# Reordering VectorE's queue in a fused attention and two-layer kernel: evacuations ahead of left-over jobs, weight sums behind the next maximum

## The chip, the cores and the metric

The kernel runs on one core of a Trainium2 chip. The time is that of one execution on the device, in microseconds (us); every kernel was run several times and medians are quoted. TensorE is called PE, VectorE DVE, ScalarE ACT, GpSimd POOL, as in the profile.

## The reference, cut to what matters

```python
# q, k, v: (8, 12, 448, 64), fp32
q_n, k_n = rmsnorm(q, g_q), rmsnorm(k, g_k)
scores = q_n @ k_n.T / sqrt(64)
attn   = softmax(scores)                 # per row, with the row's maximum taken off
x      = (attn @ v), heads side by side  # 3584 x 768
h      = x @ w_in                        # 768 x 2048
out    = max(0.01*h, h) @ w_out          # 2048 x 768
```

The kernel works through 24 units (`u` = 0 to 23), each of four heads of one batch. A unit has four stages (`d` = 0 to 3): in each, some score products and exponentials, and pieces of the two dense layers of an earlier batch, taken from a queue, so that PE has work while ACT takes exponentials. The second dense layer computes most of its output blocks with seven products in place of eight; for that it needs sums of weight blocks (`tw`, made once) and sums of activation blocks (`sa`, made for every pair of output tiles).

## The kernel before: the parts that matter

Evacuations of the dense layers' PSUM banks (DVE or ACT reads a product's result out of the bank in which it was accumulated) are not emitted at once. They are put on a list (`later`) and emitted by `flush()`, which every piece calls first. A stage also has *jobs*, small pieces of work for other engines; one is emitted behind each piece of the queue, and what is left over comes at the end:

```python
def fill(u, d, jobs):
    ...                                   # how much of the queue this stage takes
    while queue and debt[0] >= queue[0][0] * 0.5:
        c, fn = queue.pop(0)
        fn()
        debt[0] -= c
        if jobs:
            jobs.pop(0)()
    for job in jobs:                      # left-over jobs
        job()
    flush()                               # then what is pending
```

The start of a unit (abridged). `shift_max` is the DVE maximum and the diagonal `dg` made of it, `shift_mm` the small product that spreads it:

```python
qk(u, STEPS[d])
if d == 0:
    shift_max(u)                          # DVE: L219, L221
    if narrow(u - 1):
        pv_slot(u - 1)                    # PE: L326
        zcol(u - 1)                       # PE: L269
        shift_mm(u)                       # PE: L231, needs dg; then DVE L232, L240
        pv_out(u - 1); zcol_sum(u - 1)    # ACT L281; DVE L286, L287
ex(u)                                     # ACT: L201
```

The jobs that the argument touches (abridged):

```python
if d == 1:  job(prep_ssq, u + 2, ...) x2                  # DVE L142
if d == 2:  job(prep_rinv, u + 2)                         # ACT L147, L148
            job(prep_norm, u + 2, ...) x2                 # DVE L154, q then k
            job(prep_trd, u + 2)                          # transpose by DMA
if d in (1, 3) and 4 <= u < 8:
    job(weight_sum, u - 4, d // 2)                        # DVE L402, two halves
```

And four of the seven products of an output block (abridged). Products 5 and 6 accumulate onto banks that DVE has to have read in between:

```python
def i4():
    flush(); mm(bank("md"), sa[:, 2], tw[:, 2], True)
    later(lambda: add(g["o"][1][:, R], g["o"][1][:, R], "md"))   # DVE reads md, L434
def i5():
    flush(); mm(g["mc"], sa[:, 3], wblock(1, 1), False)
    ...
def i6():
    flush(); mm(g["md"], gblock(tt[1], 1), tw[:, 3], False)      # onto md again
def i0(), i2():                                                   # the same with bank ma, read at L443
    ...
```

The softmax here doesn't subtract the row's maximum and nothing guards it: scores larger than these inputs give would overflow.

## Time and profile before

| | before |
|---|---|
| median of 3 runs | 433.38 us (433.32 to 433.84) |
| span in the profile | 431.2 us |
| PE busy | 409.3 us, 95% |
| ACT, DVE busy | 306.5 us (71%), 273.2 us (63%) |
| PE waiting for DVE's diagonal (L231) | 2.4 us, 4 times |
| PE waiting for DVE's read of `md` | 1.3 us, 4 times |

How to read it: PE is the bound nearly everywhere, so only gaps in PE's own row cost time. A line of the list of waits has the engine that waits with its line, whom it waits for, then total us, number, longest. A line of a timeline has start, duration, engine, line, operation, and in brackets the idle time ahead of it and what ended it. A matmul's end is modelled, so the bracket shows less than the real gap; the distance of two starts, compared with the same pair elsewhere, shows it fully. The lines themselves stand in the prediction.

### The profile page before, as it was taken

The page shows a single profiled execution, that of the slowest core. Times are in us where ns is not written, and L with a number is a line of the kernel's source. Part 1 is how long each engine was busy: PE and PEld are TensorE (multiplying, and loading weights), DVE is VectorE, ACT ScalarE, POOL GpSimd, SP SyncE. Part 2 cuts the span into 40 slices and gives each one's busy share as a digit, 9 for nine tenths or more (in the row PEclk, how much of TensorE's full clock was granted, in tenths as well). Part 3 has the DMA queues.
Part 4 walks back from the last instruction along what each step waited for, and adds up shares of the span by engine and source line. Part 5 has one row for each costly group of instructions (what it writes and reads, how often), then busy time and mean ns, then how long its engine had stood idle before and what let it go on. Part 6 is the DMA issues. An engine that isn't in the chain of part 4 may idle for free.

```text
span 431.2 us, 8844 instructions
## 1 busy us (share of the span) xinstructions
PE 409.3 (95%) x3645; PEld 211.2 (49%) x3645; DVE 273.2 (63%) x434; ACT 306.5 (71%) x466; POOL 86.6 (20%) x77
## 2 busy tenths in 40 slices
PE   7677999999989999999999999999999999999996
PEld 6545444445444544454445544454445444455553
DVE  5898656888659865487369864587359840542162
ACT  5389888757986779966986789966986757643400
POOL 2885423300002102112102102111101101010000
PEclk9699999999999999999999999999999999999999
DMA  8999993789566896578555797488572460212013
GB/s 264 198 239 252 237 254 85 143 170 221 154 104 114 194 206 161 143 128 212 156 103 136 170 209 171 130 141 194 160 109 44 118 143 16 44 38 73 2 44 103
DMA packets 66476, 62.37 MB, mean 145 GB/s; under 512 B 35716, under 2 KB 61572, under 8 KB 66436
## 3 DMA queue, kind: packets, MB, share of 16 engines
q1 hardware_dynamic: 55840, 49.62, 46.7%
q0 software_dynamic: 10272, 11.80, 17.8%
q8 instruction: 28, 0.46, 0.4%
q10 hardware_dynamic: 324, 0.39, 0.3%
q14 instruction: 12, 0.10, 0.1%
HBM read 45.61 MB, written 11.01 MB: 131 GB/s over the span
## 4 chain that ended last, share of the span: by engine, by line
PE 63%; ACT 16%; DVE 12%; issue 3%; ACTq 0%; DVEq 0%
PE hps L347 25%; ACT et L201 8%; PE ma L427 7%; PE md L427 6%; PE sT L182 5%; PE sT L326 4%; PE op L387 4%; PE mc L427 4%; DVE n L154 3%; PE mb L427 3%; ACT gt L341 3%; PE zc L269 3%; DVE ssq L142 1%; DVE sT L219 1%; ACT x L281 1%
## 5 line engine op out<-in xcount | busy, mean ns | idle before, releaser
L201 ACT ACTIVATE et<-sT,eb 128x896 f16<-128x896 f32 x166 | 158.6, 1005 | 15.6 <-PE sT L182 13.3
L347 PE MATMUL hps<-xt,win 128*128 128x448 f16 x756 | 151.0, 353 | 0.2 <-DVE xt L335 0.2
L347 PEld LDWEIGHTS <-win 128*128 128x128 f16 x756 | 70.6, 98 | 71.4 <-issue 9.9
L341 ACT ACTIVATE gt<-hps 128x448 f16<-128x448 f32 x126 | 65.7, 541 | 20.1 <-PE hps L347 19.4
L306 POOL TENSOR_TENSOR xt<-x,rz 128x896 f16<-128x896 f32 x16 | 33.5, 2092 | 150.8 <-DMA rz<-zs 49.8
L154 DVE TENSOR_TENSOR n<-rq,rinv 128x896 f16<-128x896 f32 (+2 forms) x25 | 27.5, 1102 | 48.4 <-ACT rinv L148 44.9
L182 PE MATMUL sT<-qkT 64*64 64x448 f16 x664 | 52.6, 366 | 4.8 <-ACT et L201 4.3
L142 DVE TENSOR_REDUCE ssq<-sq 128x14 f32<-128x896 f32 (+2 forms) x49 | 50.1, 1055 | 1.2 <-ACT sq L131 1.2
L427 PEld LDWEIGHTS <-sa 128*128 128x128 f16 x352 | 32.8, 98 | 26.3 <-issue 6.1
L281 ACT COPY x<-sT 128x896 f32<-128x896 f32 x19 | 17.2, 907 | 39.5 <-DVE sT L232 39.5
L111 POOL DMA_DIRECT2D vt<-in_v_dram x24 | 18.2, 760 | 114.4 <-PE sT L326 106.9
L427 PEld LDWEIGHTS <-gt 128*128 128x128 f16 x264 | 25.2, 98 | 20.3 <-issue 4.4
L219 DVE TENSOR_REDUCE sT<-sT 128x1 f32<-128x896 f32 x22 | 24.0, 1093 | 17.5 <-PE sT L182 17.5
L182 PEld LDWEIGHTS <-qkT 64*64 64x64 f16 x672 | 15.8, 104 | 39.0 <-issue 35.9
L387 PE MATMUL op<-wout,gt 128*128 128x384 f16 x192 | 34.1, 327 | 0.0
L427 PE MATMUL ma<-wout,gt 128*128 128x384 f16 x176 | 32.3, 326 | 0.1
L154 DVE TENSOR_TENSOR n<-rk,rinv 128x896 f16<-128x896 f32 (+2 forms) x25 | 30.1, 1206 | 0.0
L326 PE MATMUL sT<-et,vt 64*64 64x448 f16 x532 | 28.5, 349 | 0.3
L408 DVE TENSOR_TENSOR sa<-gt 128x512 f16<-128x512 f16 (+1 forms) x15 | 8.1, 543 | 29.6 <-ACT gt L341 29.6
L326 PEld LDWEIGHTS <-vt 64*64 64x64 f16 x672 | 20.4, 107 | 10.8 <-issue 1.1
L387 PEld LDWEIGHTS <-gt 128*128 128x128 f16 x192 | 17.7, 98 | 14.0 <-issue 3.2
L453 ACT COPY ost<-ma 128x384 f32<-128x384 f32 x11 | 5.3, 480 | 23.6 <-PE ma L427 23.6
(87 smaller groups left out, 444.9 us busy)
## 6 DMA issues: line engine op xcount, KB each, us to landing
rq<-in_q_dram SPq DMA_DIRECT2D x24, 448.0 KB, 5.0
rk<-in_k_dram SPq DMA_DIRECT2D x24, 448.0 KB, 5.9
out_dram<-ost SPq DMA_DIRECT2D x52, 192.0 KB, 3.8
rz<-zs SPq DMA_DIRECT2D x38, 224.0 KB, 3.3
vt<-in_v_dram POOLq DMA_DIRECT2D x24, 224.0 KB, 5.0
win<-in_moe_w_in_dram POOLq DMA_DIRECT2D x8, 384.0 KB, 9.4
wout<-in_moe_w_out_dram POOLq DMA_DIRECT2D x2, 1536.0 KB, 23.7
out_dram<-ost SPq DMA_DIRECT2D x4, 96.0 KB, 2.1
```

Source lines behind the costliest of these rows:

```text
L142: nc.vector.tensor_reduce(buf(u, "ssq")[:, ti, :, c[0]:c[1]], buf(u, f"sq{ti}")[:, :, c[0]:c[1]], axis=AXL.X, op=ALU.add)
L154: nc.vector.tensor_tensor(buf(u, "n16")[:, ti, c[0]:c[1]].rearrange("p s a d -> p a s d"), src[:, :, c[0]:c[1]], buf(u, "rinv")[:, ti, :, ...
L182: nc.tensor.matmul(banks[a][64 * r:64 * r + 64, 0:S].rearrange("p (t x) -> p t x", t=NS), kT(u, r, a, t), qT(u, r, a), start=True, stop=True)
L201: nc.scalar.activation(s["et"][:, t], sT[:, :, 0:S], AF.Exp, bias=s["eb"], scale=1.0)
L219: nc.vector.tensor_reduce(s["spare"][:, 511:512], sT[:, :, 0:S], axis=AXL.XY, op=ALU.max)
L281: nc.scalar.copy(s["x32"], s["pslot"][:, :, 0:S])
L306: eng.tensor_tensor(xts[b][:, g], s["x32"], s["rz"], op=ALU.mult)
L326: nc.tensor.matmul(s["pv"][r][64 * a:64 * a + 64, 0:S], vts[u % NV][64 * r:64 * r + 64, a, t], s["et"][64 * r:64 * r + 64, t, a], start=(t ...
L341: nc.scalar.activation(dst, src, AF.Prelu, bias=0.0, scale=1.0, alpha=0.01)
L347: nc.tensor.matmul(hps[:, 0:S], win16[:, kt // 2, kt % 2, ts(ft, P)], xt[:, kt // 2, kt % 2], start=(kt == 0), stop=(kt == KT - 1))
L387: nc.tensor.matmul(op2[:, 0:HC], gt[:, ft, ds(col(t), P)], wout16[:, ft, ds(HC * half, HC)], start=(ft == 0), stop=(ft == FT - 1))
L427: nc.tensor.matmul(bank[:, 0:HC], a[:, f], b[:, f], start=(first and f == 0), stop=(f == HF - 1), skip_group_check=not first)
```

## The change

Its intent: DVE takes its queue in order, so what is emitted ahead of an urgent operation delays it. The change puts pending evacuations, on which PE may wait, ahead of left-over jobs, and takes half of each weight sum out of the place right ahead of the next unit's maximum.

```diff
@@ def fill
             if jobs:
                 jobs.pop(0)()
+        flush()
         for job in jobs:
             job()
-        flush()
@@ main loop
-                if d in (1, 3) and 4 <= u < 8:
-                    job(weight_sum, u - 4, d // 2)
+                if d == 1 and 4 <= u < 8:
+                    job(weight_sum, u - 4, 0)
+                if d == 0 and 5 <= u < 9:
+                    job(weight_sum, u - 5, 1)
```

## The prediction

> **What bounds the kernel now.** I read the page's busy shares first, then the list of who TensorE (PE) waits for, then the timelines of PE, VectorE (DVE) and ScalarE (ACT) around every PE wait. The page gives the bound:
>
> ```profile
> PE 409.3 (95%) x3645; PEld 211.2 (49%) x3645; DVE 273.2 (63%) x434; ACT 306.5 (71%) x466; POOL 86.6 (20%) x77
> PEclk9699999999999999999999999999999999999999
> PE 63%; ACT 16%; DVE 12%; issue 3%; ACTq 0%; DVEq 0%
> ```
>
> From slice 5 on PE is busy over 90%, its clock is full, and it leads the chain that ended last. The change adds and removes no instruction: the two programs have the same 7289 PE rows in the same order and the same DVE work in another order. It can only pay where PE now stands idle for DVE or ACT. That is this list:
>
> ```profile
> PE sT L182 <- ACT et L201: 4.3, 11, 0.9
> PE tp L610 <- DVE n L154: 3.7, 2, 3.0
> PE sT L231 <- DVE dg L221: 2.4, 4, 1.1
> PE md L427 <- DVE ost L434: 1.3, 4, 0.3
> ```
>
> The change touches only the last two lines. The first two are the prologue and the exponentials, whose order stays. L231 is the small product that spreads a unit's maximum, behind the DVE chain max (L219) then diagonal (L221). It stands behind that unit's first scores, the previous unit's PV and its column sums (L269). The two places where it waits long are the starts of units 6 and 8 (a unit is four heads of one batch, u = 0 to 23, in four stages):
>
> ```profile
> 89.64 0.85 PE L269 MATMUL zc<-et,onesr 128*32 128x448 f16 x16
> 91.29 0.22 PE L231 MATMUL sT<-dg,onesp 128*128 128x64 f16 x2 [0.81 <-DVE dg L221]
> 120.06 0.85 PE L269 MATMUL zc<-et,onesr 128*32 128x448 f16 x16
> 122.02 0.22 PE L231 MATMUL sT<-dg,onesp 128*128 128x64 f16 x2 [1.11 <-DVE dg L221]
> ```
>
> Matmul ends are modelled, so I take starts. Where nothing waits, L231 starts 0.78 us after L269 (138.08 to 138.86). So the real stalls are 91.29 - 89.64 - 0.78 = 0.87 us and 122.02 - 120.06 - 0.78 = 1.18 us. The same reading gives 0.12 us at unit 5 (76.86 to 77.76) and none at unit 7 (104.30 to 105.08).
>
> The fourth line is the last product of a seven-product output block. It accumulates into bank `md` that DVE must have read before:
>
> ```profile
> 149.85 1.47 PE L427 MATMUL mc<-wout,sa 128*128 128x384 f16 x8
> 151.64 1.46 PE L427 MATMUL md<-tw,gt 128*128 128x384 f16 x8 [0.32 <-DVE ost L434]
> 150.03 1.08 DVE L154 TENSOR_TENSOR n<-rk,rinv 128x896 f16<-128x896 f32 x1
> 151.03 0.55 DVE L434 TENSOR_TENSOR ost<-md,ost 128x384 f32<-128x384 f32 x1
> ```
>
> The DVE read ends at 151.58 and `md` starts at 151.64. Elsewhere the same pair of products starts 1.30 us apart (235.73 and 237.03), here 1.79, so the stall is 0.49 us. It occurs four times, at 151.6, 198.4, 295.1 and 345.2 (units 10, 13, 19, 22). The normalisation of k (L154) sits in front of the read only because it was emitted first.
>
> **What the Trainium skill says.** "Perfetto Trace Analysis", section "Identifying the Most-Contended Engine", says that matmul busy share does not measure the distance to the roofline, because matmuls are pipelined. The trace agrees: weight loads are 49% beside matmuls' 95%. So I count starts, not busy time. "PSUM — Partial Sum Buffer", section "Engine vs sequencer instructions", says that the queues of ScalarE, VectorE and GpSimd are strictly first in, first out and that matmuls start in program order; the `md` read behind L154 is just that. The same page, "PSUM bank collisions raise a hardware error", says that two engines must not touch one bank and quadrant at once; here `md` starts 0.06 us after the read ends. "SBUF — State Buffer", section "SBUF: two separate sides", says that GpSimd and a VectorE operation with two SBUF inputs share a port pair held for a whole instruction, and that the later one is fully blocked. The trace agrees: a weight sum (L402) takes 0.95 us alone but 1.66 us from 83.44 to 85.10, while GpSimd runs 82.61 to 84.29.
>
> **The change part by part.**
>
> (a) *Weight sums.* Eight instructions of 0.95 us (0.86 from start to next start). The four second halves leave the end of stage 3, ahead of the maxima of units 5, 6, 7 and 8, and go into stage 0 of those same units, after the maximum and the column-sum additions.
>
> Unit 5: the maximum goes from 76.29 to about 75.7, when its scores are ready, but L231 then waits for L269: gain 0.12 us.
>
> Unit 6: here DVE is the bound. From 80.62 to the diagonal at 90.95 its instructions stand practically back to back. The sum taken from 88.50 is balanced by the one now inserted at 81, in front of the same stretch. What is saved is only part of the port blocking: the sum at 83.44 starts 0.75 us later, GpSimd also moves, by 0.74 (its square waits for the reduction L142), and the sum ends at about 85.8 instead of 85.1. The maximum comes at 89.7 instead of 89.83. PE keeps nearly its whole 0.87 us stall. Units 5 and 6 together: 0.1 us.
>
> Unit 7: DVE had 0.51 us idle at 97.9 that takes up part of the insertion, and PE did not stall: 0.
>
> Unit 8: DVE is idle 4.27 us ahead of 115.21, so the sum inserted at 107 is free, and the one removed at 119.02 is a real saving:
>
> ```profile
> 115.21 1.09 DVE L154 TENSOR_TENSOR n<-rq,rinv 128x896 f16<-128x896 f32 x1 [4.27 <-ACT rinv L148]
> 119.02 0.95 DVE L402 TENSOR_TENSOR tw<-wout,tw 128x1536 f16<-128x1536 f16 x1
> 120.55 1.09 DVE L219 TENSOR_REDUCE sT<-sT 128x1 f32<-128x896 f32 x1
> ```
>
> The maximum moves to 119.69, the diagonal ends at about 121.1, L231 starts at about 121.16. Gain 0.86 us, with 0.32 of the 1.18 left. The fourth sum, now at about 124 in unit 8, falls into 4.02 us of DVE idle ahead of 129.45.
>
> (b) *Evacuations first.* In units 10, 13, 16, 19 and 22 the read of `md` now stands ahead of the normalisation of k. It starts about 1.0 us earlier (150.03) and ends at 150.6, before PE asks at 151.15. Four stalls of 0.49 us go: 1.96 us. Unit 16 has no such stall, since its `md` falls after the next maximum. The normalisation comes 0.46 us later, but feeds only a transpose for two units ahead.
>
> (c) *What the same edit costs.* In units 14 and 20 the pended sums of activations (L408, L411), which wait for ACT, now stand ahead of the second square reduction (L142, 1.00 us start to start), and so that reduction lies between them and the read of bank `ma`:
>
> ```profile
> 226.56 0.42 DVE L408 TENSOR_TENSOR sa<-gt 128x512 f16<-128x512 f16 x1 [3.08 <-ACT gt L341]
> 227.55 0.56 DVE L443 COPY ost<-ma 128x384 f32<-128x384 f32 x1
> 228.02 1.87 DVE L414 TENSOR_TENSOR sa<-gt 128x512 f16<-128x512 f16 x1
> ```
>
> The reduction would start at 227.35, the read at 228.35 and end at 228.90. PE wants `ma` again at 228.65: a stall of 0.3 us. Unit 8 shows that picture already: read 131.25, product 131.85 where 130.26 + 1.30 = 131.56 was due. Twice that is 0.6 us lost. The rest of the DVE delay vanishes: L414, 1.87 us long, is blocked by GpSimd until 229.6 anyway, so it ends at the same time, and the following maximum is not delayed.
>
> Sum: 0.1 + 0.86 + 1.96 - 0.6 = 2.3 us. 433.38 - 2.3 = 431.1.
>
> **The rivals.**
>
> *All four boundaries pay.* The naive count is that each removed sum moves its maximum by 0.86 us. For it: the chain of waits passes through L402 ahead of unit 6. Against it: the insertion into the same DVE-bound stretch, and no stall at unit 7. The most it could pay at unit 6 is its 0.87; then the time is about 430.3.
>
> *The delay is passed on.* In units 14 and 20 the reduction, moved out of 3.08 us of idle time into a busy DVE stretch, would delay the maxima of units 15 and 21 by up to 1.0 us each, if the GpSimd block did not absorb it. The profile shows the diagonal ready (235.56) only 0.1 us before PE wants it (235.66), so there is no room otherwise. Together with a gain at unit 8 that another wait takes over, the time would be about 433.
>
> *PE stalls vanish but ACT becomes the bound.* At units 10 and 22 ACT has over 2 us of idle time ahead of its next unit's first copy (2.74 us at 156.11), which speaks against it. It would leave about half of (b): 432.
>
> **Range and chances.** Each stall is counted directly and is small; no item alone can move the time by 2% (8.7 us), and all addressable stalls together are under 5 us. The three runs of before lie within 0.5 us. I take 430.2 to 432.4: the lower end is unit 6 paying too, the upper is half of the gain lost. Faster by over 2%: 1%; within 2%: 98%; slower by over 2%: 1%.
>
> **What would show it right or wrong.** Right: the line for `md` vanishes from PE's waits; L231 waits about 0.2 to 0.3 us at unit 8 and still about 0.7 to 0.8 at unit 6; two new waits of about 0.3 us for the `ma` copy in units 14 and 20 (perhaps visible only in starts 1.6 us apart instead of 1.3); DVE busy time unchanged near 273. Wrong: unit 6's stall gone, L231 waits of near 1 us at units 15 and 21, or a new wait of PE for ACT.

## The result, and the profile after

The changed kernel took 431.35 us (430.36 to 431.62, 4 runs), the kernel before 433.35 us in the runs then at hand (432.62 to 433.84, 4 runs). The ratio is 0.9953, with a 95% interval of 0.9937 to 0.9968. Ratios here are the mean time of one kernel's fast runs over that of the other's fast runs of the same rounds, so not quite the ratio of the medians.

The waits of PE in the profile of the changed kernel, the line that is left of the two that the change addresses:

```profile
PE sT L231 <- DVE dg L221: 1.5, 4, 0.8
```

The line for `md` is gone. The 1.5 us are these places and two small ones (units 12 and 18); first the start of unit 6, then of unit 8, in PE's timeline:

```profile
89.92 0.85 PE L269 MATMUL zc<-et,onesr 128*32 128x448 f16 x16
91.58 0.22 PE L231 MATMUL sT<-dg,onesp 128*128 128x64 f16 x2 [0.81 <-DVE dg L221]
...
120.46 0.85 PE L269 MATMUL zc<-et,onesr 128*32 128x448 f16 x16
121.55 0.22 PE L231 MATMUL sT<-dg,onesp 128*128 128x64 f16 x2 [0.24 <-DVE dg L221]
```

Start to start, less the usual 0.78 us, the stall at unit 6 is 91.58 - 89.92 - 0.78 = 0.88 us (0.87 before) and at unit 8 0.31 us (1.18 before). The first of the four former `md` stalls, PE then DVE:

```profile
149.37 1.47 PE L427 MATMUL mc<-wout,sa 128*128 128x384 f16 x8
150.68 1.46 PE L427 MATMUL md<-tw,gt 128*128 128x384 f16 x8
...
149.55 0.55 DVE L434 TENSOR_TENSOR ost<-md,ost 128x384 f32<-128x384 f32 x1
150.02 1.08 DVE L154 TENSOR_TENSOR n<-rk,rinv 128x896 f16<-128x896 f32 x1
```

The two products now start 1.31 us apart instead of 1.79: the read starts 1.1 us ahead of the product that needs it. And the price, in unit 14, where the reduction of the squares now runs between the sums of activations and the read of bank `ma`:

```profile
225.97 1.46 PE L427 MATMUL mb<-tw,sa 128*128 128x384 f16 x8
227.58 1.46 PE L427 MATMUL ma<-wout,gt 128*128 128x384 f16 x8
...
225.98 1.08 DVE L142 TENSOR_REDUCE ssq<-sq 128x14 f32<-128x896 f32 x1
226.98 0.55 DVE L443 COPY ost<-ma 128x384 f32<-128x384 f32 x1
```

`mb` and `ma` start 1.61 us apart where 1.30 is normal, with no bracket on `ma`, since the modelled end of `mb` (225.97 + 1.46 = 227.43) nearly covers the gap: the list of waits does not show this loss at all.

**A better ruler than the whole time.** The start of the dense layers' first long product (L347, bank `hps`) comes at 49.20 us in the profile of before and between 48.71 and 50.72 us in the ten profiles. In that prologue PE waits for input and normalisation; in the changed kernel's profile it had already lost 0.40 us there, though the code up to there is the same. I therefore compare the *steady part*, from that start to the end of PE's last matmul: 377.91 us before, 375.77 us after, a difference of 2.14 us. The start of L231 in each unit, counted from the same point, tells where it comes from (in us, against before, good to 0.02 since the rows of a timeline are rounded; the rows name the units at whose L231 a step shows):

| at L231 of unit | change | evacuations alone | sums alone | first sum stays | sums into idle | three more moves |
|---|---|---|---|---|---|---|
| 5 | -0.12 | -0.01 | -0.12 | -0.01 | -0.12 | -0.12 |
| 6 | -0.11 | -0.01 | -0.11 | -0.88 | -0.99 | -0.99 |
| 7 | 0.00 | -0.02 | -0.01 | -0.76 | -0.98 | -0.98 |
| 8 | -0.87 | -0.04 | -0.89 | -1.64 | -1.86 | -2.17 |
| 10 | -1.36 | -0.53 | -0.90 | -2.12 | -2.35 | -2.65 |
| 13 | -1.77 | -1.02 | -0.89 | -2.58 | -2.79 | -3.36 |
| 15 | -1.46 | -0.72 | -0.89 | -2.27 | -2.80 | -3.36 |
| 19 | -1.97 | -1.21 | -0.92 | -2.80 | -3.29 | -4.18 |
| 21 | -1.67 | -0.91 | -0.93 | -2.50 | -3.30 | -4.19 |
| 22 | -2.15 | -1.40 | -0.94 | -2.98 | -3.78 | -4.67 |
| end | -2.14 | -1.39 | -0.93 | -2.97 | -3.77 | -4.66 |

### The profile page after: what moved, and what is told of

Read it like the earlier page. It is cut to its first block, busy times and chain, and to the rows that moved or that the text cites. A ratio compares the mean times of both kernels' runs of the same rounds, so it can differ in the third digit from the quotient of the medians.

```text
span 429.5 us, 8844 instructions
## 1 busy us (share of the span) xinstructions
PE 409.5 (95%) x3645; PEld 211.3 (49%) x3645; DVE 272.1 (63%) x434; ACT 306.5 (71%) x466; POOL 86.5 (20%) x77
## 4 chain that ended last, share of the span: by engine, by line
PE 64%; ACT 17%; DVE 10%; issue 2%; DMA 1%; SPq 0%; ACTq 0%; DVEq 0%
PE hps L347 23%; ACT et L201 8%; PE md L427 7%; PE mc L427 7%; PE sT L182 6%; PE ma L427 6%; PE sT L326 5%; ACT gt L341 4%; PE op L387 3%; PE zc L269 3%; PE mb L427 2%; DVE n L154 2%; ACT x L281 1%; DVE ssq L142 1%; ACT zs L292 1%
## 5 line engine op out<-in xcount | busy, mean ns | idle before, releaser
L347 PE MATMUL hps<-xt,win 128*128 128x448 f16 x756 | 151.1, 353 | 0.2 <-DVE xt L335 0.2
L347 PEld LDWEIGHTS <-win 128*128 128x128 f16 x756 | 70.6, 98 | 71.5 <-issue 10.1
L306 POOL TENSOR_TENSOR xt<-x,rz 128x896 f16<-128x896 f32 x16 | 33.5, 2091 | 150.1 <-DMA rz<-zs 49.1
L154 DVE TENSOR_TENSOR n<-rq,rinv 128x896 f16<-128x896 f32 (+2 forms) x25 | 29.0, 1164 | 47.8 <-ACT rinv L148 44.3
L154 DVE TENSOR_TENSOR n<-rk,rinv 128x896 f16<-128x896 f32 (+2 forms) x25 | 28.9, 1156 | 0.0
```

The costliest lines, as they stand in the source:

```text
L154: nc.vector.tensor_tensor(buf(u, "n16")[:, ti, c[0]:c[1]].rearrange("p s a d -> p a s d"), src[:, :, c[0]:c[1]], buf(u, "rinv")[:, ti, :, ...
L306: eng.tensor_tensor(xts[b][:, g], s["x32"], s["rz"], op=ALU.mult)
L347: nc.tensor.matmul(hps[:, 0:S], win16[:, kt // 2, kt % 2, ts(ft, P)], xt[:, kt // 2, kt % 2], start=(kt == 0), stop=(kt == KT - 1))
```

## The experiments

Eight kernels (the last is the changed kernel once more) were run in two sets of four, each set beside the kernel before on one chip, in five rounds. All gave correct results. The steady part of before comes from a single profile; as a check on it, "read later", whose code is that of before up to unit 9, stays within 0.04 us of it there.

| run | median us | before, same rounds | ratio (95%) | steady part against before |
|---|---|---|---|---|
| evacuations alone | 431.94 | 433.88 | 0.9958 (0.9943 to 0.9974) | -1.39 |
| sums alone | 431.97 | 433.88 | 0.9954 (0.9940 to 0.9969) | -0.93 |
| no evacuations first in stage 1 | 430.46 | 433.88 | 0.9922 (0.9906 to 0.9938) | -2.79 |
| first sum stays | 430.72 | 433.88 | 0.9925 (0.9906 to 0.9944) | -2.97 |
| sums into idle | 429.77 | 433.71 | 0.9911 (0.9897 to 0.9924) | -3.77 |
| read later | 436.05 | 433.71 | 1.0051 (1.0038 to 1.0064) | +2.24 |
| three more moves | 428.87 | 433.71 | 0.9884 (0.9869 to 0.9899) | -4.66 |
| the change again | 431.40 | 433.71 | 0.9941 (0.9929 to 0.9954) | -2.12 |

### Each half alone

Evacuations alone, against the kernel before:

```diff
+        flush()
         for job in jobs:
             job()
-        flush()
```

> Only the evacuations go ahead of the left-over jobs; the weight sums stay as in the kernel before. My theory: the four waits of TensorE for the read of bank md go (4 x 0.48 = 1.9 us), the two new delays of the ma product in units 14 and 20 come (2 x 0.31 = 0.6 us), the stalls at units 6 (0.87) and 8 (1.18) stay. Net 1.3 us less than before, about 432.0 us. Rival (the weight sums carry the whole gain): the same as before, 433.3 us.

Sums alone: the other half of the diff, with `flush()` behind the jobs as before.

> Only the second halves of the weight sums move; evacuations stay behind the left-over jobs. My theory: unit 8's stall falls from 1.18 to about 0.3 us, unit 5 gains 0.12, unit 6 keeps its 0.87, unit 7 loses about 0.1; the md waits of 0.49 us stay at all four places. Net 0.9 us less than before, about 432.4 us. Rival (each maximum freed pays 0.86 us): 2 us or more less, 431.3 us.

Evacuations alone shortened the steady part by 1.39 us (1.3 expected): four steps of -0.48 to -0.49, behind units 9, 12, 18 and 21, and two of +0.30, at units 15 and 21. Units 6 and 8 stayed as before; the start of unit 8 in its PE timeline:

```profile
121.56 0.85 PE L269 MATMUL zc<-et,onesr 128*32 128x448 f16 x16
123.50 0.22 PE L231 MATMUL sT<-dg,onesp 128*128 128x64 f16 x2 [1.09 <-DVE dg L221]
```

Sums alone gave 0.93 us (0.9 expected), practically all of it at unit 8 (unit 5's 0.12 us were lost again at unit 7), and left `md` where it was:

```profile
148.75 1.47 PE L427 MATMUL mc<-wout,sa 128*128 128x384 f16 x8
150.53 1.46 PE L427 MATMUL md<-tw,gt 128*128 128x384 f16 x8 [0.31 <-DVE ost L434]
```

That is 1.78 us from start to start, the stall of before. The rival of "sums alone", 2 us or more, looks right by the whole time (431.97 against 433.88) and wrong by the steady part, which is the same program from unit to unit. The two parts' steady gains add to 2.32 us against 2.14 for both together; their whole times add to nearly twice what the change gave. So the difference of whole times is about 1 us too good for the steady part of "sums alone". The profiled prologues account for only 0.2 us of it (48.99 against 49.20). Most of the rest lies with the kernel before: its profile has a span of 431.2 us, but its 11 executions in this set have 431.4 to 433.3, median 432.1, while those of "sums alone" (429.8 to 430.6, median 430.2) agree with their profile's 430.1. Where the kernel before spends those 0.9 us stays open, for only the one execution of it was kept as a profile. It is a warning for reading differences under 1 us in this kernel from whole times.

### The reduction in units 14 and 20

```diff
-        flush()
+        if d != 1:
+            flush()
         for job in jobs:
             job()
+        flush()
```

> The changed kernel, but in stage 1 of each unit the evacuations stay behind the left-over jobs, so that in units 14 and 20 the square reduction again runs in the idle time ahead of the sums of activations. My theory: the second ma product starts 1.30 us after mb instead of 1.61 in both units, all else as in the changed kernel: 0.6 us less than it, about 430.7 us. Rival (the reduction's delay is absorbed and costs nothing): the same as the changed kernel.

The steady part was 0.65 us shorter than the changed kernel's (375.12 against 375.77), and the median 430.46 us. Unit 14 in PE's timeline:

```profile
226.21 1.46 PE L427 MATMUL mb<-tw,sa 128*128 128x384 f16 x8
227.51 1.46 PE L427 MATMUL ma<-wout,gt 128*128 128x384 f16 x8
```

1.30 us, as expected; the steps of +0.31 and +0.30 at units 15 and 21 are absent. So this price of the change is real, although no wait in the list names it.

### Why unit 6 gained nothing

The prediction's claim is that DVE in unit 5 is full from end to end, so that a weight sum taken away ahead of unit 6's maximum and another put in some 7.5 us earlier cancel. To test it, the one put in is taken back to its old place:

```diff
+                if d == 3 and u == 4:
+                    job(weight_sum, 0, 1)
-                if d == 0 and 5 <= u < 9:
+                if d == 0 and 6 <= u < 9:
                     job(weight_sum, u - 5, 1)
```

> The changed kernel, but the second half of the first weight sum stays where it was, at the end of unit 4. My theory: VectorE's back-to-back stretch in unit 5 is then 0.86 us shorter, so that TensorE's wait for the diagonal at unit 6 (0.81 us) falls to under 0.1 us; unit 5 loses its 0.12 us again. Net 0.7 us less than the changed kernel, about 430.6 us. Rival (something other than VectorE's order holds unit 6, for example ScalarE or the transposes): the wait at unit 6 stays near 0.8 us and the time is as in the changed kernel.

The start of unit 6 in PE's timeline:

```profile
89.13 0.85 PE L269 MATMUL zc<-et,onesr 128*32 128x448 f16 x16
89.92 0.23 PE L231 MATMUL sT<-dg,onesp 128*128 128x64 f16 x2
```

The stall is gone, 0.79 us from start to start. Unit 5 loses its 0.12 us again, and the steady part ends 0.83 us shorter than the changed kernel's. The rival, that something else holds unit 6, falls: no instruction of ACT and no transpose was moved. This run also shows that undoing a quarter of one part of a change can be worth nearly as much as the whole part (0.83 us here, 0.93 for sums alone).

### The read of bank md, made later

The other direction: the kernel before, with one reduction more on DVE ahead of that read. The result goes nowhere.

```diff
+    def pad():
+        nc.vector.tensor_reduce(scr, wout16[:, 0, 0:512], axis=AXL.X, op=ALU.max)
@@
+                if d == 2 and u in (9, 12, 18, 21):
+                    job(pad)
```

> The kernel before with one extra VectorE reduction (128x512, about 0.6 us) behind the normalisation of k in units 9, 12, 18 and 21, that is ahead of the read of bank md; its result is not used. My theory (TensorE is held by that read and by nothing else): the four stalls grow from 0.49 us each by the start-to-start time of the extra reduction, about 0.6, so the time grows by 2.4 us, to about 436 us. Rival (the wait is shadowed by another one of like length, and the gain of the change came from elsewhere): less than 1 us more.

DVE and PE at the first of the four places (line numbers are one higher in this kernel):

```profile
151.79 0.68 DVE L558 TENSOR_REDUCE scr<-wout 128x1 f32<-128x512 f16 x1
152.39 0.55 DVE L435 TENSOR_TENSOR ost<-md,ost 128x384 f32<-128x384 f32 x1
...
150.61 1.47 PE L428 MATMUL mc<-wout,sa 128*128 128x384 f16 x8
152.99 1.46 PE L428 MATMUL md<-tw,gt 128*128 128x384 f16 x8 [0.91 <-DVE ost L435]
```

The products are now 2.38 us apart, 0.59 more than before, and the reduction takes 0.60 us from its start to the next start. Four times that is 2.4; the steady part grew by 2.24 us and the median came to 436.05 (2.4 and about 436 expected). So PE is held by that read and nothing shadows it.

### A version that beats both kernels

If the argument is right, the weight sums belong into DVE's idle stretches in units 7 and 8; they are first read by the product into `mb` in unit 8's stage 2, at 128.76 in this variant's profile.

```diff
-                if d == 1 and 4 <= u < 8:
-                    job(weight_sum, u - 4, 0)
-                if d == 0 and 5 <= u < 9:
-                    job(weight_sum, u - 5, 1)
+                for n, x in {(4, 1): ((0, 0),), (7, 0): ((0, 1), (1, 0)), (7, 1): ((1, 1), (2, 0)),
+                             (8, 0): ((2, 1), (3, 0), (3, 1))}.get((u, d), ()):
+                    job(weight_sum, n, x)
```

together with the condition `d != 1` of above.

> All weight sums but the first leave units 4 to 6 and go into VectorE's idle stretches of units 7 and 8 (two at the start of unit 7, two in its stage 1, three at the start of unit 8); in stage 1 evacuations stay behind the left-over jobs. My theory: unit 6's stall of 0.87 us and unit 7's new 0.1 us go, the ma delays of units 14 and 20 do not come, unit 8 keeps about 0.3 us. From the first product of the second layer to the end 3.8 us shorter than before and 1.7 us shorter than the changed kernel; time about 429.7 us. Rival (the sums delay unit 8's maximum or the first products that read them, in unit 8): a new wait at or after unit 8 and no more gain than the variant in which the first sum stays.

The steady part was 3.77 us shorter than before, 3.8 expected. Two lines of DVE's timeline show the idle stretches still there, only shorter, in units 7 and 8:

```profile
114.57 1.09 DVE L154 TENSOR_TENSOR n<-rq,rinv 128x896 f16<-128x896 f32 x1 [2.22 <-ACT rinv L148]
...
127.94 0.42 DVE L408 TENSOR_TENSOR sa<-gt 128x512 f16<-128x512 f16 x1 [1.40 <-ACT gt L341]
```

Before they were 4.27 and 4.02 us. What PE still waited for were the diagonals of units 8, 12 and 18, each behind sums of activations that nothing needs so early. In the last variant these are emitted later too:

```diff
-            for n, x, fs in (..., (10, 0, (s3, s4)), ...):
+            for n, x, fs in (..., (11, 0, (s3, s4)), ...):
@@
-                std[1] = also(std[1], lambda: later(s2, tt))
-                std[2] = also(std[2], lambda: later(s3, tt), lambda: later(s4, tt))
+                std[2] = also(std[2], lambda: later(s2, tt), lambda: later(s3, tt), lambda: later(s4, tt))
```

> The variant with the sums in the idle stretches, and further the activations' sums that stand ahead of the maxima of units 8, 12 and 18 behind them. My theory: the left stalls of the diagonal go too, 0.3 us at unit 8, 0.2 at unit 12, 0.3 at unit 18: 0.8 us less than that variant, 4.6 less than before from the first product of the second layer on; about 428.9 us. Rival (the moved sums then hold the products that read them): waits of TensorE for those sums and no gain.

PE at the start of unit 8:

```profile
119.83 0.85 PE L269 MATMUL zc<-et,onesr 128*32 128x448 f16 x16
120.60 0.23 PE L231 MATMUL sT<-dg,onesp 128*128 128x64 f16 x2
```

L231 stands in none of this kernel's waits of PE. Unit 8's L231 comes 0.31 us earlier than in "sums into idle"; from one unit's L231 to the next, the steps against before are -0.23 at unit 12 and -0.35 at unit 18; no new wait came. A stall that no list names and no variant touched is still there: in unit 8 `mb` and `ma` start 1.58 us apart (128.85 and 130.43), as in all ten profiles to within 0.02. Median 428.87 us against 433.71, ratio 0.9884: more than twice the gain of the change, with the same instructions.

> The changed kernel again, beside the three others on the same chip: 2.1 us less than before from the first product of the second layer to the end; any difference of the whole time beyond that is the prologue's.

The changed kernel again had 431.40 us and a steady part 2.12 us shorter than before. Its own profile is 0.15 us behind the first one at unit 6. There the transposed input landed 6.4 us after its issue, at about 82.5, and not 5.7 us after as in the first profile, at about 81.7; so the scaling that reads it (L138) started 1.00 us after the inserted weight sum instead of 0.87, and the stall at unit 6 was 1.03 us. Most of this is made up at unit 12, where the first profile lost 0.08 us (see below), so the equal total at the end is partly luck. Steps of this size are not resolved by one profile.

## Why the prediction was right

Time: 431.1 was predicted, with 430.2 to 432.4; 431.35 and later 431.40 were measured. By its own steps:

1. *Only PE's gaps count, and the change can close only those of L231 and `md`.* Right. Evacuations alone, sums alone and the later read all moved the steady part by what those gaps moved.
2. *Unit 8: 0.86 us.* Right: 0.87, and 0.31 of the stall left (0.32 predicted).
3. *Units 5 and 6: 0.1 together.* Right in the first profile: 0.12 and -0.01; in the repeat unit 6 lost 0.16 us, 0.13 of it to the late transpose. That unit 6 gains nothing because DVE is full is shown, not only argued: with the first sum back in its old place, unit 6's stall vanished.
4. *Unit 7: 0.* Off by 0.11 us, a loss. It lies in the first-layer products in front of unit 7: with the sum inserted into unit 6, the multiplication that makes `xt` (L306) ends at 102.54, and the fifth of the six products that start at 101.72, the first to read that part of `xt`, was due at 102.48 and started at 102.60. All five profiles with that sum in unit 6 have this delay, and none of the other five. I had looked only at the diagonal there.
5. *Evacuations: four times 0.49.* Right in size: 0.48 to 0.49 each. In the naming I erred: the four stalls at the times given lie in stage 2 and 3 of units 9, 12, 18 and 21, not 10, 13, 19 and 22, and the one that has no stall is in unit 15, not 16. The times, and so the sum, are not affected. Two smaller slips: the page counts 3645 matmuls and 3645 weight loads, 7290 rows and not 7289, and slice 12 of PE's row shows an 8, so PE is not over 90% busy in every slice from 5 on. Nothing rests on either.
6. *Units 14 and 20: twice 0.3 lost.* Right: 0.31 and 0.30 in the changed kernel, absent when stage 1 is excepted. The rival, that the delay goes on to the next maximum, did not occur, and for the reason predicted: the sum L414 behind the read took 1.10 us in place of 1.87. GpSimd's multiplication (L306) ran for another 1.58 us after its start before the change (228.02 to 229.60) and for 0.82 us after it (227.44 to 228.26).
7. *The sum: 2.3.* The steady part gave 2.14. Of the missing 0.16, 0.11 is unit 7; another 0.08 came at unit 12, where the diagonal's wait was 0.23 us against 0.15. This is not the change's: a normalisation ahead of the diagonal (L154, at 179.31) met GpSimd's multiplication (L306), the port sharing that the prediction describes. That multiplication started 8.49 us after unit 11's L231 and the normalisation took 1.34 us; before it was 8.41 and 1.25, and in the changed kernel run again 8.38 and 1.24, without the loss. Why it started later in that one execution is not shown.

ACT did not become the bound, the third rival: PE's waits for its exponentials were 4.2 us after and 4.3 before.

## What to carry to other kernels

On an in-order engine that is full between two urgent operations, moving work from just ahead of the second to just behind the first gains nothing; look for the nearest real idle stretch, and move it there. A rule such as "evacuations first" helps where the other engine waits for the evacuation and costs where the evacuation's list itself waits for something: check each place where the order changes. When gains are of the order of 0.5%, compare the starts of one recurring instruction in the bound engine's timeline, counted from a point behind the prologue, rather than whole times or the list of waits.

## What the Trainium skill lacked or had wrong

- "Perfetto Trace Analysis", section "Identifying the Most-Contended Engine", says that pipelined PE instructions look smaller in the trace. Here a record looks longer than its share: a 128x384 product is given 326 ns, while eight of them start 1.30 us before the next group, 163 ns each. The advice not to trust matmul busy time holds, but the reason shows itself the other way round, and a stall of 0.31 us (unit 14) disappears under it without any wait listed. That section does not say to use the distance of starts, which shows it (1.61 us for 1.30).
- "PSUM — Partial Sum Buffer", section "PSUM bank collisions raise a hardware error", says that engines must be kept apart per bank and quadrant, but not what the handover costs. Here PE's next product into the bank started 0.06 us after DVE's read ended (151.58 to 151.64), and 0.05 us in the variant with the later read (152.94 to 152.99).
- No page says how far one kernel's prologue can spread from run to run: here the same code reached its first long product at 48.71 to 50.72 us in ten profiles.
